# Two linear-attention blocks mixed by a gate: a second key unit by seven products, and three first products put together in PSUM

## The chip, the cores and the metric

One Trainium2 chip; the kernel uses one of its cores. The metric is the device time of one execution in microseconds (us). A core has a matrix engine (TensorE, PE in the profile, with its weight loads as PEld), a vector engine (VectorE, DVE), an activation engine (ScalarE, ACT), a general one (GpSimd, POOL) and a queue processor (SyncE, SP) that issues most transfers. Matrix products are accumulated in PSUM, which has eight banks of 512 float32 columns here; everything else that is worked on lies in SBUF.

## The reference, cut to what matters

```
x: [2048, 640] bf16,  wqkv: [640, 1920],  wo: [640, 640]   (one wqkv, wo for block A, one for block B)
g = sigmoid(x @ gate_w)                                     # one number per row
block: q, k, v = split(x @ wqkv), 32 heads of 20
       phi(t) = where(t > 0, t + 1, exp(t)) + 1e-6          # = min(exp(t), 1) + max(t, 0) + 1e-6
       kv = phi(k)^T v per head,  z = sum over rows of phi(k)
       o  = (phi(q) kv) / (phi(q) z + 1e-6)
       out = o @ wo
result = g * blockA(x) + (1 - g) * blockB(x)
```

Both blocks read the same x. The kernel never forms v: it computes phi(k)^T x (called G here), multiplies that by the value weights and by wo to get one small matrix per block, and applies it to the scaled phi(q).

## The kernel before, in words

x is 16 row tiles of 128. Because the two blocks are added up at the end, many pairs of products have the form of a 2 x 2 block product, and the kernel computes such a block product with seven products instead of eight (a Strassen form). It pays with sums of operands (on DVE, before the products) and sums of results (on DVE and ACT, between the products, because the PSUM sums are copied out, added and used again).

The stages, in the order of the matrix queue:

1. K: keys. For a tile and a block, five steps (one per 128 rows of the weights) of two matmuls each, 512 and 128 or 129 columns (`k_step`, lines 652 and 653). After the two blocks of a tile, `k_post` makes phi: ACT takes exp (line 700) and for block B also the exp of the gate column (691), DVE takes min and adds EPS (703), and then either ACT takes relu (712, 727) and DVE adds (718, 730), or DVE does both at once from PSUM (739). Which of the two is listed by hand in `RELUB` and `KRS`. Tiles 0 to `KT`-1 run in order ahead of everything; the others by the list `MAIN`. Two tiles, 2*`KU` and 2*`KU`+1, are done as one unit by seven products (`ks_unit`, lines 817 to 842); its operand sums are `kw_sums` (768, of the weights) and `kx_sums` (789, of x).
2. G: phi(k)^T x in five units (`g_unit`, products at line 1166), each by seven products named 1, 2, 5, 6, 3, 7, 4; products 1 and 2 are cut before the last pair of tiles, whose parts are steps 8 and 9. The sums over keys are made by `s_pair` (889), those over x by `t_all` (914), into the buffer TX.
3. Q and R: queries (lines 1045, 1134), Q by seven products, R directly; phi again (1075, 1078, 1088, 1090, 1092, 1145 to 1152). `QD` and `RD` list where DVE takes max and sum at once.
4. kv, wp, den: small products that make the per-block matrices and the denominators, as transfers allow.
5. O: output (line 1556), eight units by seven products, with stores.

The order of the matrix queue is the list `MAIN`, written out. A token K14A is tile 14, block A; K6.5 is product 5 of the unit of tiles 12 and 13; G3.8 is step 8 of G unit 3. DVE, ACT and the queues take their order from a planner (`Sched`) that places each operation by estimated costs when the program is built; PSUM banks and other slots are given out there too. Every operation waits on semaphores for what it reads and for the former users of its slot. A matmul that must wait holds up everything behind it, since that queue is strictly in order.

In a seven-product unit the first product serves two results. In the units of K, Q and O, ACT copies it from its PSUM bank into a second bank (for keys line 842), and the second product is accumulated there on top. In the G units of the kernel before, ACT copies it to SBUF (1194), the second product has a bank of its own, and DVE adds the two (1199).

Of the kernel before, what the change touches and what calls it, by code (L numbers as in the profile page):

```python
# [11 lines left out]
D = 640  # L12
# [31 lines left out]
HC = 320  # L44
NPU = 5
SSB = 20480
RELUB = (3, 5, 7, 9, 11, 13)
KT = 10
KU = 6
KJ = 7  # L50
KWT = 5
KRS = ("10A", "10B", "11A", "11B", "12A", "13B", "14A", "14B", "15A", "15B", "8A", "9A", "9B",)
MAIN = """K6.1 K14A K6.5 K6.2 K6.6 K14B K6.3 K6.7 K10A K10B K6.4 K11A K11B K15A K15B G3.1 G3.8 G1.1 G2.1 G0.1
G3.2 G2.8 G1.8 G1.2 G1.9 G3.9 G0.2 G0.8 G0.9 G2.2 G0.5 G0.6 G1.5 G0.3 G0.7 G1.6 G3.6 G0.4 G2.9 G2.6
G2.5 Q4.1 G1.7 G1.3 G3.5 G2.7 G1.4 Q4.6 Q4.5 G2.3 Q4.2 Q4.7 G3.3 Q4.3 G2.4 Q1.1 Q0.1 kvA X2 Q1.6
Q0.5 G3.7 Q0.2 Q0.6 Q4.4 Q1.5 Q0.7 Q1.2 G4.1 Q0.3 G4.8 Q1.7 G3.4 Q3.1 Q2.1 Q1.3 G4.2 Q3.6 Q1.4 G4.6
Q3.2 Q2.5 Q2.6 Q2.2 G4.9 Q0.4 Q3.5 Q2.3 G4.5 Q3.7 Q2.7 G4.7 Q2.4 Q3.4 G4.3 G4.4 Q3.3 wA0 dA0 R4B
wA1 LA dB0 S1 S0 kvB R4A wB0 R1A R2B R2A wB1 T1 R3A R0.1 R1B R3B R0.6 R0.5 O2.1
O3.5 R0.7 R0.2 O1.1 R0.3 O0.1 O2.2 O1.2 R0.4 O0.2 O3.1 O2.6 O1.6 O3.2 O0.5 O3.6 O3.3 O1.5 O1.7 dA1
dB1 S3 S2 O1.3 O2.5 O3.7 O2.7 O2.3 O3.4 O1.4 O2.4 O0.6 O0.3 O4.1 O7.1 O6.1 O0.7 O4.2 O5.1 O6.2  # L60
O7.2 O5.2 O4.5 O4.6 O5.5 O6.5 O5.6 O4.7 O6.6 O0.4 O6.3 O6.7 O4.3 O7.6 O7.5 O5.7 O5.3 O7.7 O7.3 O4.4
O5.4 O6.4 O7.4"""
RS = (0,)
# [247 lines left out]
def body(nc, A_x, A_wqkv, A_wo, B_x, B_wqkv, B_wo, gate_w, out, log=None):  # L311
# [463 lines left out]

    def kx_sums():
        t1, t2 = 256 * KU, 256 * KU + 128
        a11, a12, a21, a22 = [XT[:, c : c + 2, lo : lo + 128] for lo in (t1, t2) for c in (0, 2)]
        for k, in0, in1, need in (
            (1, a21, a22, ()),  # L780
            (2, a11, KX[1], (1,)),
            (5, XT[:, 4, t1 : t1 + 128], XT[:, 4, t2 : t2 + 128], ()),
            (3, a21, a11, ()),
            (4, a12, KX[2], (2,)),
        ):
            bkx[k] = Buf("kx")
            op(
                "DVE",
                lambda e, k=k, in0=in0, in1=in1: e.tensor_tensor(out=KX[k], in0=in0, in1=in1, op=ALU.subtract),
                dve2(128 if k == 5 else 256),  # L790
                ins=[bxt[2 * KU], bxt[2 * KU + 1]] + [bkx[j] for j in need],
                outs=[bkx[k]],
                name="kx",
            )
# [7 lines left out]
    def ks_unit(j):  # L802
# [36 lines left out]
        def step(n):  # L839
            if n == 1:  # L840
                mm(px, D + 1, True, [(WK["A"][:, c, :], xt(c, 0)) for c in range(2)], bx + [bwk["A", c] for c in range(2)] + [bwz])
                d[1] = op("ACT", lambda e: e.activation(psw(py, D), psw(px, D), ACT.Copy), act_cost(D), ins=[px], outs=[py], name="kfk")
            elif n == 2:
                mm(py, D, False, [(WK["A"][:, c, :], xt(c, 0)) for c in range(2, 5)], bx + [bwk["A", c] for c in range(2, 5)])
            elif n == 5:
                mm(pz, D + 1, True, [(KW[1][:, c, :], KX[1][:, c, :]) for c in range(2)] + [(WK["B"][:, 4, :], xt(4, 1))], bx + [bkw[1], bkx[1], bwk["B", 4], bgc])
                d[5] = save(s5, pz, True)
            elif n == 6:
                mm(px, D + 1, False, [(KW[2][:, c, :], KX[2][:, c, :]) for c in range(2)], [bkw[2], bkx[2]], [d[1]])
                d[2] = save(s2, px, False)  # L850
            elif n == 3:
                mm(pz, D + 1, False, [(WK["B"][:, 2 + c, :], KX[4][:, c, :]) for c in range(2)] + [(WK["B"][:, 4, :], KX[5])], [bkx[4], bkx[5], bgc] + [bwk["B", c] for c in range(2, 5)], [d[5]])
                comb(pz, s2, False)
                k_post(t1, [("A", py, "%dA" % t1 in KRS), ("B", pz, "%dB" % t1 in KRS)])
            elif n == 7:
                mm(px, D + 1, False, [(KW[3][:, c, :], KX[3][:, c, :]) for c in range(2)], [bkw[3], bkx[3]], [d[2]])
# [48 lines left out]
    def t_all(j0, j1):  # L905
        xi = bxn[2 * j0 : 2 * j1] + [bxo]

        def tt(k, in0, in1, how, need):
            b = Buf("tx%d" % k)
            for j in range(j0, j1):  # L910
                bt[k, j] = b
            s_op.append(op(
                "DVE",
                lambda e: e.tensor_tensor(out=tk(k), in0=in0, in1=in1, op=how),
                dve2((j1 - j0) * LW),
                ins=xi + [bt[n, j0] for n in need],
                outs=[b],
                name="tx",
            ))
# [30 lines left out]
    for t in range(2, KT):  # L950
# [3 lines left out]
        if t == KWT:  # L954
            kw_sums()
    t_all(0, 8)
    kx_sums()
    bgt, gtx = Buf("gtx"), []
# [72 lines left out]
    def qu_unit(p, g):  # L1031
# [33 lines left out]
        def post(X, h, pv, ins):  # L1065
# [8 lines left out]
            one = ["%d.%d%s%d" % (p, g, X, i) in QD for i in range(2)]  # L1074
            o = [op("ACT", lambda e: e.activation(EQ[:, eq.slot + h, :], pv(), ACT.Exp), act_cost(512), ins=ins, outs=[eq], name="qe")]  # L1075
            rel = dst = PQ[X, b][:, g, :]
            if not one[h]:
                o.append(op("ACT", lambda e: e.activation(rel, pv(), ACT.Relu), act_cost(512), ins=ins, outs=[pq], after=home, name="qr"))
            n = 1
            if not any(one):  # L1080
                n, dst = 2, PP[X, p][:, g, :, :]
            if any(one) or two is not None:
# [3 lines left out]

                e2 = Buf("eq2")
                op("DVE", lambda e: e.tensor_scalar(ev(), ev(), 1.0, EPS, op0=ALU.min, op1=ALU.add), dve4(512 * n), ins=[eq], outs=[e2], name="qt")
                if one[h]:
                    o.append(op("DVE", lambda e: e.scalar_tensor_tensor(dst, pv(), 0.0, ev(), op0=ALU.max, op1=ALU.add), dve1(512), ins=ins + [eq, e2], outs=[pqf], after=home, name="qs"))  # L1090
                else:
                    op("DVE", lambda e: e.tensor_tensor(out=dst, in0=dst, in1=ev(), op=ALU.add), dve2(512 * n), ins=[pq, eq, e2], outs=[pqf], name="qs")
            qu_ops[p].extend(o)
# [82 lines left out]
    def g_unit(g):  # L1176
# [454 lines left out]
    kleft = len([t for t in MAIN.split() if t[0] == "K"])  # L1631
    ks, kps, ktiles, kdone = ks_unit(KU), {}, set(), {j for j in (1, 3, 5) if 2 * j + 1 < KT}
    for tok in MAIN.split():
        sch.base = None if tok[0] == "K" else 10**5
        if tok[0] == "K":
            if tok[2] == ".":
                ks(int(tok[3]))
                if tok[3] == "4":
                    ktiles |= {2 * KU, 2 * KU + 1}
            else:  # L1640
# [4 lines left out]
                if X == "B":  # L1645
                    k_post(t, [(Y, kps[Y, t], "%d%s" % (t, Y) in KRS) for Y in XS])
                    ktiles.add(t)
            kleft -= 1
            for j in (3, 5):
                if 2 * j >= KT - 2 and j not in kdone and all(t < KT or t in ktiles for t in range(2 * j - 2, 2 * j + 2)):  # L1650
# [87 lines left out]
```

## Time and profile before

| | |
|---|---|
| median of 3 runs | 175.97 us (175.24 to 176.11) |
| the profiled execution: its time | 175.2 us |
| its span (first to last instruction) | 173.8 us |
| PE busy | 171.3 us, 1331 matmuls |
| DVE busy | 140.1 us, 246 instructions |
| ACT busy | 115.3 us |
| POOL busy | 5.3 us |
| clock granted to PE | 1.00 |

The span is what the profile covers; 1.4 us of the execution's own time lie outside it. Busy times are sums of the durations as recorded. Neighbours on an engine overlap a little (a matmul's record reaches over the start of the next), so the distance between two starts, not the duration, is what one costs on a full queue. Times of day in a trace count from the span's start.

### The profile page before, as it was taken

How to read it: one execution, taken by the hardware profiler on the slowest of the kernel's cores; microseconds unless marked ns; L12 is line 12 of the kernel's file. 1: busy time of each engine (PE TensorE's matmuls, PEld its weight loads, DVE VectorE, ACT ScalarE, POOL GpSimd, SP SyncE). 2: the span in 40 equal slices, each digit the busy share in tenths (PEclk: the TensorE clock that was granted, in tenths of full speed). 3: DMA queues.
4: the chain of work that ended last, by engine and by line, in shares of the span. 5: the costliest groups of instructions: out<-in, count | busy, mean ns of one | idle time of the engine just before them, and what ended most of it. 6: DMA issues, size and time to landing. Idle time of an engine off the chain costs nothing.

```text
span 173.8 us, 3365 instructions
## 1 busy us (share of the span) xinstructions
PE 171.3 (99%) x1331; PEld 107.6 (62%) x1331; DVE 140.1 (81%) x246; ACT 115.3 (66%) x221; POOL 5.3 (3%) x17
## 2 busy tenths in 40 slices
PE   9999999999999999999999999999999999999995
PEld 4555555555577777666566565655556667777773
DVE  2275999999999958559959889799999985899550
ACT  4378888999933332467599597956898864456324
POOL 2000000000000170000000000000000000000000
PEclk9999999999999999999999999999999999999999
DMA  6969999980000025138818003277670002460125
GB/s 187 324 122 179 220 373 366 347 160 5 0 4 0 0 42 98 38 75 72 188 20 220 4 0 75 59 204 198 232 191 3 0 3 69 115 204 4 47 102 191
DMA packets 33035, 20.59 MB, mean 118 GB/s; under 512 B 18260, under 2 KB 32892, under 8 KB 33020
## 3 DMA queue, kind: packets, MB, share of 16 engines
q1 hardware_dynamic: 32062, 19.76, 44.5%
q10 hardware_dynamic: 958, 0.63, 1.2%
q8 instruction: 10, 0.16, 0.4%
q14 instruction: 5, 0.04, 0.1%
HBM read 10.88 MB, written 4.26 MB: 87 GB/s over the span
## 4 chain that ended last, share of the span: by engine, by line
PE 99%; ACT 0%; issue 0%; DVE 0%
PE ps L1166 22%; PE ps L1556 22%; PE ps L652 18%; PE ps L1045 13%; PE ps L1134 10%; PE ps L653 5%; PE ps L817 3%; PE ps L579 1%; PE ps L1420 1%; PE ps L1346 1%; PE ps L1314 1%; PE ps L592 1%; ACT PKS L1621 0%; DVE ONE L477 0%; PE ps L629 0%
## 5 line engine op out<-in xcount | busy, mean ns | idle before, releaser
L652 PE MATMUL ps<-WKW,XT 128*128 128x512 bf16 x140 | 38.9, 381 | 0.0
L653 PE MATMUL ps<-WKW,XT 128*128 128x128 bf16 (+1 forms) x140 | 30.7, 219 | 0.0
L700 ACT ACTIVATE EKT<-ps 128x640 bf16<-128x640 f32 x31 | 21.9, 716 | 4.6 <-PE ps L653 4.1
L652 PEld LDWEIGHTS ps<-WKW,XT 128*128 128x128 bf16 x140 | 13.7, 98 | 16.6 <-DMA WKW<-in_A_wqkv_dram 0.4
L1166 PE MATMUL ps<-TX,PKS 128*128 128x321 bf16 (+1 forms) x160 | 23.8, 300 | 0.0
L1166 PEld LDWEIGHTS ps<-TX,PKS 128*128 128x128 bf16 x160 | 15.7, 98 | 7.2
L1166 PE MATMUL ps<-XN,PKS 128*128 128x321 bf16 (+1 forms) x120 | 18.2, 300 | 0.0
L1194 ACT ACTIVATE EKT<-ps 128x321 f32<-128x321 f32 (+1 forms) x15 | 6.4, 438 | 16.6 <-PE ps L1166 9.9
L1166 PEld LDWEIGHTS ps<-XN,PKS 128*128 128x128 bf16 x120 | 11.7, 98 | 5.5
L653 PEld LDWEIGHTS ps<-WKW,XT 128*128 128x128 bf16 x140 | 13.7, 98 | 0.0
L1075 ACT ACTIVATE EQ<-ps 128x512 bf16<-128x512 f32 x18 | 10.8, 601 | 3.7 <-PE ps L1045 2.9
L889 DVE TENSOR_TENSOR PKS<-PKS 128x1280 bf16<-128x1280 bf16 (+2 forms) x20 | 12.9, 683 | 0.0
L712 ACT ACTIVATE PKS<-ps 128x640 bf16<-128x640 f32 x16 | 11.4, 722 | 0.0
L703 DVE TENSOR_SCALAR EKT<-EKT 128x1280 bf16<-128x1280 bf16 (+1 forms) x19 | 8.2, 435 | 3.7 <-ACT EKT L700 3.6
L1145 ACT ACTIVATE EQ<-ps 128x1024 bf16<-128x1024 f32 x8 | 8.2, 1028 | 4.3 <-PE ps L1134 3.6
L1045 PE MATMUL ps<-XT,WQA 128*128 128x512 bf16 x36 | 10.4, 379 | 0.0
L1579 DVE TENSOR_TENSOR PKS<-ps,PKS 128x320 bf16<-128x320 f32 x11 | 5.4, 490 | 5.2 <-PE ps L1556 4.9
L1199 DVE TENSOR_TENSOR WKW<-ps,EKT 128x320 bf16<-128x320 f32 x15 | 7.2, 486 | 2.8 <-PE ps L1166 2.6
L1134 PE MATMUL ps<-XT,WQA 128*128 128x512 bf16 x40 | 9.4, 381 | 0.0
L1134 PE MATMUL ps<-XT,WQB 128*128 128x512 bf16 x40 | 9.2, 380 | 0.0
L1572 ACT ACTIVATE PKS<-ps 128x320 f32<-128x320 f32 x11 | 4.8, 441 | 5.9 <-PE ps L1556 5.9
L739 DVE SCALAR_TENSOR_TENSOR PKS<-ps,EKT 128x640 bf16<-128x640 f32 x10 | 8.2, 820 | 0.1
(179 smaller groups left out, 321.9 us busy)
## 6 DMA issues: line engine op xcount, KB each, us to landing
out_dram<-PKS SPq DMA_DIRECT2D x15, 160.0 KB, 1.8
XN<-in_A_x_dram SPq DMA_DIRECT2D x1, 2240.0 KB, 9.1
WKW<-in_A_wqkv_dram SPq DMA_DIRECT2D x5, 160.0 KB, 3.7
WKW<-in_B_wqkv_dram SPq DMA_DIRECT2D x5, 160.0 KB, 3.6
WQA<-in_A_wqkv_dram SPq DMA_DIRECT2D x1, 800.0 KB, 10.8
WQB<-in_B_wqkv_dram SPq DMA_DIRECT2D x1, 800.0 KB, 12.0
WVA<-in_A_wqkv_dram SPq DMA_DIRECT2D x1, 800.0 KB, 12.0
PKS<-in_B_wqkv_dram SPq DMA_DIRECT2D x1, 800.0 KB, 5.2
```

Source lines behind the costliest of these rows:

```text
L652: e.matmul(a[:, 0:512], l, WK[X][:, c, 0:512], start=(c == 0), stop=(c == NC - 1))
L653: return e.matmul(a[:, 512:w], l, WK[X][:, c, 512:w], start=(c == 0), stop=(c == NC - 1))
L700: op("ACT", lambda e, i=i, ps=ps: e.activation(evg(i), psg(ps), ACT.Exp), act_cost(D), ins=[ps] + first, outs=[ek, b], name="ke")
L703: lambda e: e.tensor_scalar(EK[:, ek.slot : ek.slot + n, :], EK[:, ek.slot : ek.slot + n, :], 1.0, EPS, op0=ALU.min, op1=ALU.add),
L712: op("ACT", lambda e, X=X, ps=ps: e.activation(pkt(X, t), psg(ps), ACT.Relu), act_cost(D), ins=[ps], outs=[rk], name="kr")
L739: lambda e, X=X, i=i, ps=ps: e.scalar_tensor_tensor(pkt(X, t), psg(ps), 0.0, evg(i), op0=ALU.max, op1=ALU.add),
L889: lambda e: e.tensor_tensor(out=out, in0=a, in1=b, op=ALU.subtract),
L1045: r = e.matmul(PS[:, ps.slot, :], w, x, start=(first and i == 0), stop=(i == len(prs) - 1), skip_group_check=not first)
L1075: o = [op("ACT", lambda e: e.activation(EQ[:, eq.slot + h, :], pv(), ACT.Exp), act_cost(512), ins=ins, outs=[eq], name="qe")]
L1134: r = e.matmul(PS[:, ps.slot + h, :], WQ[X][:, c, g::5], XT[:, c, 1024 + 512 * h : 1536 + 512 * h], start=(c == 0), stop=(c == NC - 1))
L1166: r = e.matmul(PS[:, ps.slot, 0:w], reg[:, j, :], mov(j, w), start=(first and j == 0), stop=(j == 7), skip_group_check=not first)
L1556: r = e.matmul(PS[:, ps.slot, 0:HALF], reg(g), mov(g), start=(first and g == 0), stop=(g == NC - 1), skip_group_check=not first)
```

## The change

- A second unit of keys by seven products: `KU` becomes (3, 6), so that tiles 6 and 7 are done like 12 and 13. `KT` falls from 10 to 4: tiles 0 to 3 run ahead, tiles 4 to 15 by `MAIN`, whose first line now begins with tiles 4, 5 and unit 3. The sums of x get a set of buffers per unit (`KX[u, k]`) and are queued after tile `KXT[u]` = 3; those of the weights after tile `KWT` = 2 instead of 5.
- `t_all`, the sums of x behind TX, is queued at the token `TXT` = K15B in two halves (eight operations of 4 x 322 columns a row instead of four of 8 x 322), and waits for the last key operation of DVE that stands before it there.
- In the G units in `FK` = (0, 1, 2), product 1 is copied by ACT from PSUM into the bank of product 2 (1274 in the changed file), product 2 runs undivided at step 9 on top of it (step 2 is empty), and ACT copies the result out (1279); DVE's addition is gone in these three.
- In the query units the wait of DVE's min step and of its addition is narrowed: where a half is done alone, it waits for the exp and relu of that half, not for both.
- The lists of who does max and sum (`RELUB`, `KRS`, `QD`, `RD`) and `MAIN` are new. The G and O products, R and the small products keep their number and sizes.

```
-KT = 10
-KU = 6
+KT = 4
+KU = (3, 6,)
-KWT = 5
+TXT = "K15B"
+FK = (0, 1, 2,)
+KXT = {3: 3, 6: 3}
+KWT = 2
-MAIN = """K6.1 K14A K6.5 K6.2 K6.6 K14B K6.3 K6.7 K10A K10B K6.4 K11A K11B K15A K15B G3.1 G3.8 G1.1 G2.1 G0.1
-G3.2 G2.8 G1.8 G1.2 G1.9 G3.9 G0.2 G0.8 G0.9 G2.2 G0.5 G0.6 G1.5 G0.3 G0.7 G1.6 G3.6 G0.4 G2.9 G2.6
...
+MAIN = """K4A K5A K3.1 K5B K3.2 K3.5 K3.6 K4B K3.7 K3.3 K10A K3.4 K8A K8B K15A K10B K15B K11A K6.1 K14A
+K6.5 K6.2 K6.6 K11B K6.3 K9A K6.7 K9B K14B K6.4 G1.1 G1.2 G0.1 G0.2 G2.1 G2.2 G0.8 G1.8 G2.8 G3.1
+G0.9 G3.2 G2.9 G1.9 G0.5 G0.6 G3.8 G3.9 G1.5 G0.3 G2.6 G1.6 G3.6 G1.3 G0.7 G2.5 G0.4 G1.7 G2.3 G3.5
...
-QD = ("0.0A0", "0.0A1", "0.1B0", "0.1B1", "0.2A0", "0.2B0", "0.2B1", "0.3A0", "1.0B1",)
-RD = ("A0", "A1", "A4", "B0",)
+QD = ("0.0A0", "0.0A1", "0.0B0", "0.1B0", "0.1B1", "0.2A0", "0.2B0", "0.3A0", "0.3B1", "0.4A1", "0.4B1", "1.0B1",)
+RD = ("A0", "A1", "A3", "A4", "B0",)
...
+                after=pk_last[-1:],
                 name="tx",
...
-    t_all(0, 8)
-    kx_sums()
+        for u in KU:
+            if t == KXT[u]:
+                kx_sums(u)
...
-                e2 = Buf("eq2")
-                op("DVE", lambda e: e.tensor_scalar(ev(), ev(), 1.0, EPS, op0=ALU.min, op1=ALU.add), dve4(512 * n), ins=[eq], outs=[e2], name="qt")
+                e2, mine = Buf("eq2"), [ex] if any(one) else exs
+                q = [op("DVE", lambda e: e.tensor_scalar(ev(), ev(), 1.0, EPS, op0=ALU.min, op1=ALU.add), dve4(512 * n), ins=mine, outs=[e2], name="qt")]
...
+        if g in FK:
+            py.need = HC
...
-            if n in (2, 9):
+            if n in (2, 9) and g not in FK:
                 prod(g, "P2", py, ra2, xv(1, False), HC, True, lambda j: xn(j, 1) + [bpk[one[0], 2 * j + 1]], js=(0, KJ) if n == 2 else (KJ, 8))
             if n == 8:
-                d["s1"] = save(t1, px, HC, "p1s")
+                if g in FK:
+                    d["s1"] = op("ACT", lambda e: e.activation(PS[:, py.slot, 0:HC], PS[:, px.slot, 0:HC], ACT.Copy), act_cost(HC), ins=[px], outs=[py], name="p1f")
+                else:
+                    d["s1"] = save(t1, px, HC, "p1s")
+            elif n == 9 and g in FK:
+                prod(g, "P2", py, ra2, xv(1, False), HC, False, lambda j: xn(j, 1) + [bpk[one[0], 2 * j + 1]])
+                op("ACT", lambda e: e.activation(GT[:, ga.slot, 0:HC], PS[:, py.slot, 0:HC], ACT.Copy), act_cost(HC), ins=[py], outs=[ga], prio=-2, name="c11")
             elif n == 9:
                 comb(ga, 0, py, t1, "c11")
...
+            if tok == TXT:
+                t_all(0, 4)
+                t_all(4, 8)
```

More of the change, by code (lines that the diff above doesn't have):

```diff
@@ L855, in step @@
             elif n == 7:
-                mm(px, D + 1, False, [(KW[3][:, c, :], KX[3][:, c, :]) for c in range(2)], [bkw[3], bkx[3]], [d[2]])
+                mm(px, D + 1, False, [(KW[3][:, c, :], KX[j, 3][:, c, :]) for c in range(2)], [bkw[3], bkx[j, 3]], [d[2]])
                 d[7] = comb(px, s5, True)
@@ L1085, in ev @@
                     return EQ[:, eq.slot : eq.slot + 2, :] if n == 2 else EQ[:, eq.slot + h, :]
[L1087 to L1088 removed]
+                e2, mine = Buf("eq2"), [ex] if any(one) else exs
+                q = [op("DVE", lambda e: e.tensor_scalar(ev(), ev(), 1.0, EPS, op0=ALU.min, op1=ALU.add), dve4(512 * n), ins=mine, outs=[e2], name="qt")]
                 if one[h]:
[L1090 to L1092 removed]
+                    q.append(op("DVE", lambda e: e.scalar_tensor_tensor(dst, pv(), 0.0, ev(), op0=ALU.max, op1=ALU.add), dve1(512), ins=ins + [e2], outs=[pqf], after=home, name="qs"))
+                    o.append(q[1])
+                else:
+                    q.append(op("DVE", lambda e: e.tensor_tensor(out=dst, in0=dst, in1=ev(), op=ALU.add), dve2(512 * n), ins=[rl if any(one) else pq, e2], outs=[pqf], name="qs"))
+                for x in q:
+                    x.ins.append(eq)
+                    eq.readers.append(x)
             qu_ops[p].extend(o)
@@ L1647, in body @@
                     ktiles.add(t)
+            if tok == TXT:
+                t_all(0, 4)
+                t_all(4, 8)
             kleft -= 1
-            for j in (3, 5):
+            for j in (1, 3, 5):
                 if 2 * j >= KT - 2 and j not in kdone and all(t < KT or t in ktiles for t in range(2 * j - 2, 2 * j + 2)):
```

63 lines of the change are left out of this document (35 added, 28 removed).

## The prediction

> **What bounds the kernel now.** I read the page first: span, busy time, clock and chain.
>
> ```profile
> span 173.8 us, 3365 instructions
> ...
> PE 171.3 (99%) x1331; PEld 107.6 (62%) x1331; DVE 140.1 (81%) x246; ACT 115.3 (66%) x221; POOL 5.3 (3%) x17
> ...
> PEclk9999999999999999999999999999999999999999
> ...
> PE 99%; ACT 0%; issue 0%; DVE 0%
> ```
>
> The chain that ended last is matmuls almost throughout, at full granted clock. A busy matmul engine could still hide waits, so next come the waits of PE:
>
> ```profile
> PE ps L579 <- DVE ONE L477: 0.3, 1, 0.3
> ```
>
> That is its only row: after the first 0.3 us no matmul waited for another engine. So every matmul that is taken away shortens the span by its distance to the next one, and every new wait of a matmul lengthens it, one for one. The price of a key step is in the timeline of PE (start, duration):
>
> ```profile
> 4.37 0.38 PE L652 MATMUL ps<-WKW,XT 128*128 128x512 bf16 x1
> ...
> 24.84 0.38 PE L652 MATMUL ps<-WKW,XT 128*128 128x512 bf16 x1
> ...
> 30.29 0.38 PE L652 MATMUL ps<-WKW,XT 128*128 128x512 bf16 x1
> ```
>
> Between the last two lie 20 steps (a 512- and a 128-column matmul each): 5.45 / 20 = 0.2725 us a step. Last, the helpers, by stage (span, then PE, PEld, DVE and ACT busy):
>
> ```profile
> 12.30:31.30 19.00, 19.00 (x141) 10.76 (x140) 16.63 (x29) 16.63 (x32) 0.00 (x0) 1.00 1.06 281
> 31.30:47.10 15.80, 15.80 (x117) 8.94 (x116) 15.71 (x26) 15.36 (x31) 0.00 (x0) 1.00 0.47 121
> 47.10:57.00 9.90, 9.90 (x75) 7.13 (x74) 9.65 (x17) 3.62 (x9) 0.00 (x0) 1.00 0.01 2
> ...
> 79.70:130.00 50.30, 50.30 (x443) 29.74 (x443) 45.26 (x81) 40.36 (x66) 0.25 (x2) 1.00 0.52 123
> ```
>
> The keys end at 47.1. Until 31.3 DVE and ACT have room (16.6 of 19.0); from there to 47.1 both are full; in the first products of G ACT is nearly free.
>
> **The change, part by part.** *Matmuls.* Tiles 6 and 7 took 2 tiles x 2 blocks x 5 = 20 steps; by seven products they take 2+3+3+2+3+2+3 = 18. That is 4 matmuls fewer (1327 against 1331), 2 x 0.2725 = 0.545 us. The other products keep number and width: step 9 of a forked G unit runs the eight matmuls that steps 2 and 9 had. The switches between products of different tile shapes are as many as before. So the gain has a hard top: 0.54 us, 0.31%. (The Trainium skill, "TensorE: Matmul & The Clock Gate", section "Back-to-back issue gap", gives 131 and 81 ns as the sustained distance of 512- and 128-column matmuls with weight loads. By it the gain would be an estimated 2 x 0.212 = 0.42 us; this trace, with 0.2725 a pair, doesn't agree.)
>
> *What the second unit puts on ACT and DVE*, by groups of one shape (count, busy, mean ns), with the pieces that the new lists move:
>
> ```profile
> L712 ACT ACTIVATE PKS<-ps 128x640 bf16<-128x640 f32 x16 | 11.4, 722 | 0.0
> ...
> L1078 ACT ACTIVATE PQ<-ps 128x512 bf16<-128x512 f32 x6 | 3.6, 594 | 0.0
> ...
> L1194 ACT ACTIVATE EKT<-ps 128x320 f32<-128x320 f32 x5 | 2.0, 438 | 4.6 <-DVE PKS L718 3.0 <-PE ps L1166 1.5
> ...
> L842 ACT ACTIVATE ps<-ps 128x640 f32<-128x640 f32 x1 | 0.7, 726 | 0.0
> L823 ACT ACTIVATE PQ<-ps 128x645 f32<-128x645 f32 x1 | 0.7, 717 | 0.0
> ```
>
> ```profile
> L889 DVE TENSOR_TENSOR PKS<-PKS 128x1280 bf16<-128x1280 bf16 x12 | 9.6, 817 | 0.0
> ...
> L1199 DVE TENSOR_TENSOR WKW<-ps,EKT 128x320 bf16<-128x320 f32 x15 | 7.2, 486 | 2.8 <-PE ps L1166 2.6
> ...
> L914 DVE TENSOR_TENSOR TX<-XN 128x2576 bf16<-128x2576 bf16 x2 | 3.0, 1494 | 0.0
> ...
> L1090 DVE SCALAR_TENSOR_TENSOR PQ<-ps,EQ 128x512 bf16<-128x512 f32 x4 | 2.8, 692 | 0.1
> ...
> L830 DVE TENSOR_TENSOR ps<-ps,PQ 128x641 f32<-128x641 f32 x1 | 0.8, 833 | 0.1
> ...
> L789 DVE TENSOR_TENSOR PQ<-XT 128x256 bf16<-128x256 bf16 x2 | 0.6, 284 | 0.0
> ```
>
> ACT gets three copies (2.2) and two more relus of keys (1.4). DVE gets two additions (1.7), four sums of 256 columns and one of 128 (1.3). None of it is in front of PE unless a queue runs late; that is worked out below.
>
> *TX sums behind the keys.* Four of 1.49 become eight halves. I take 0.82 each, from the nearest row (1280 columns, L889), so 0.6 more in all; from below, half of 1.49, nothing more. Six stand before the last key steps, two behind. From the min step of tile 9 to the 1024-column sum that G1.5 reads, DVE has nine key steps, two halves and nine pair sums. By the L889 row scaled to their widths, and less the 0.08 by which neighbours overlap, they cost 3.9 + 1.5 + 4.3 = 9.8 us. PE has 10.9 from G1.1 to G1.5: ten products and five single steps, 80 matmuls at 0.137:
>
> ```profile
> 47.16 2.08 PE L1166 MATMUL ps<-XN,PKS 128*128 128x321 bf16 x14
> ```
>
> ((2.08 - 0.30) / 13 = 0.137.) Both start near 46.6: about 1 us to spare, so I take nothing; if DVE comes 1 us late there, each further us is paid in full.
>
> *Forks in G.* Three copies into PSUM in place of three to SBUF (0.44 either way), three additions of 0.49 off DVE, three copies out (0.44) on ACT, in the stage where ACT is busy 3.6 of 9.9. G0.8's copy has 1.2 us until G0.9 (one product, two single steps). Zero; without that cover, up to 3 x 0.44.
>
> *Queries.* Three relus (0.59) leave ACT and three max-and-sums (0.69) come to DVE, with more but shorter min steps and one such exchange of double width in R: some 2.5 us more on DVE, in a stage of 50.3 us where it was busy 45.3, 2.8 less on ACT. I take zero: no matmul waited there, and the narrowed waits let DVE start earlier. How near one came is seen in the next two rows, an exp that ends at 132.05 and the matmuls that take over its bank 0.16 later, unhindered:
>
> ```profile
> 130.99 1.06 ACT L1145 ACTIVATE EQ<-ps 128x1024 bf16<-128x1024 f32 x1
> ...
> 132.21 0.84 PE L1556 MATMUL ps<-PKS,PQ 128*128 128x320 bf16 x5
> ```
>
> *Transfers.* The orders of SP and POOL hardly change. K3.1 needs tiles 6 and 7 at 17.7, nearly 3 us earlier than their direct steps did. Their transfer is the first of the two issues in the first row (the queue's timeline), and takes 5.6 to land (the tile's view at 10.5): 16.1. Hidden by 1.6.
>
> ```profile
> 10.51 5.74 SPq L445 DMA_TRANSPOSE XT<-in_A_x_dram  x2
> ```
>
> ```profile
> DMA to landing us min/median/max: 5.6/5.6/5.6
> ```
>
> *The tight place: ACT between 12.5 and 28.* Unit 3 now stands where ACT had its room. Block B of tile 8 (K8B) takes the bank that block B of tile 7 leaves, once its exp is read. Before K8B stand 87 steps: 4.37 + 87 x 0.2725 = 28.1. ACT, from the gate column of tile 2 (same place in both programs) to that exp, has 24 instructions of 640 to 645 columns and 6 gate columns. Their distances:
>
> ```profile
> 12.53 0.17 ACT L691 ACTIVATE GE<-ps 128x1 f32<-128x1 f32 x1
> ...
> 15.25 0.17 ACT L691 ACTIVATE GE<-ps 128x1 f32<-128x1 f32 x1
> 15.32 0.70 ACT L712 ACTIVATE PKS<-ps 128x640 bf16<-128x640 f32 x1
> ...
> 32.23 0.71 ACT L700 ACTIVATE EKT<-ps 128x640 bf16<-128x640 f32 x1
> 32.81 0.73 ACT L842 ACTIVATE ps<-ps 128x640 f32<-128x640 f32 x1
> 33.48 0.70 ACT L700 ACTIVATE EKT<-ps 128x640 bf16<-128x640 f32 x1
> 34.08 0.70 ACT L712 ACTIVATE PKS<-ps 128x640 bf16<-128x640 f32 x1
> ```
>
> 0.07 a gate column; 0.58, 0.67 and 0.60 for the wide ones, where 0.67 is the copy into PSUM. With 0.60: 12.53 + 24 x 0.60 + 6 x 0.07 + 0.1 (the last one's duration beyond its distance) = 27.4. To that come five short pauses in which the next input isn't there yet, 0.1 to 0.2 each by the places of the matmuls (tile 3's first block, tiles 4 and 5 first, tile 5's second, and DVE's addition after K3.7), 0.7 in all: 28.1. It meets the matmul exactly. K3.7, five us earlier, and K15A and K10B, right after, come out with 0.1 to 0.3 to spare by the same count. I put the waits at 0.2 us: between 0 (at 0.58 a piece) and 1.2 (at 0.67, where the pauses go and the later ones follow). Queued behind such a wait is the whole matmul queue.
>
> **Sum** against the profiled execution: 173.8 - 0.54 + 0.2 = 173.5 span, 174.9 with the 1.4 around it. Its own time, 175.2, is the lowest of those shown; the median is 175.97. On the median the same -0.34 gives 175.6.
>
> **Rivals.** (1) *No wait at all.* The count above is rough by 0.1 to 0.2, and the room of 0.16 in the R stage speaks for it: -0.54, 175.4 on the median. (2) *Slower: ACT becomes the bound between 12.5 and 33.* Place: the banks of K8B, K15A and K10B. Price: with 0.67 for each wide one, 24 x 0.67 + 0.5 + 12.53 = 29.1 against 28.1; ten more wide ones until 33 add 0.3 to 0.5. Net -0.54 + 1.4 = +0.9: 176.9. It decides from 0.54 us of waits up, 0.02 a piece over my 0.60. Against it: distances of 0.58 and 0.60 are the rule in the rows, 0.67 the exception. (3) *The clock.* Many short waits could drop the granted clock. The start shows what that costs:
>
> ```profile
> 3.88 0.59 PE L652 MATMUL ps<-WKW,XT 128*128 128x512 bf16 x1
> ```
>
> 0.59 instead of 0.38 from 4.37 on; the slow stretch reaches from 0.3 to 4.3, and 4 us at half rate cost 2: 177.6 on the median. Against it: the granted clock is 9 in all 40 slices. (This is the rule of the Trainium skill, "TensorE: Matmul & The Clock Gate", section "A second HAM failure mode: psum-queue depth-cycling": short idling between groups of matmuls makes the clock swing between half and full. No run here shows it yet.) (4) *The second unit saves nothing* can't be: four matmuls are gone, and none waited.
>
> **How the numbers follow.** Forecast 0.57, rival 1 0.20, rival 2 0.20, rival 3 0.03. About 0.5% (0.88 us) is what a measurement of this kernel can tell from no change: its three runs span 0.87. Faster by more than that needs the whole gain and luck of the runs: a third of rival 1 and a seventh of the forecast, 0.15. Slower: three quarters of rival 2 and rival 3, 0.18. The same: 0.67. The range goes from the lowest run less the whole gain (175.24 - 0.54 = 174.7, rounded down to 174.6) to rival 2, 176.9.
>
> **What would show it.** Right: 1327 matmuls; the first of G's products at 46.6 to 46.9 instead of 47.16; PE's waits with a row or two of at most 0.2 by ACT at L658 between 23 and 31; none by DVE before G1.5. Wrong: waits of PE on ACT above 0.6 in sum (rival 2), a wait by TX or pair sums between 55 and 62, waits in the query stage where I took none, or a slice of the granted clock below 9 (rival 3).

## The result and the profile after

The changed kernel takes 175.34 us (median of 22 executions, 174.87 to 175.89) and the kernel before, run beside it, 175.81 (22 executions, 175.24 to 176.11). The ratio is 0.9977, 95% interval 0.9967 to 0.9987: 0.4 us or 0.23% faster, by this document's bound of 0.5% no change. The forecast was 175.6, which is 0.34 us less than a median before of 175.97; beside the 175.81 measured here it is 175.47. 0.4 us less were found, with the interval from 0.23 to 0.58.

The page of the changed kernel: span, busy times, granted clock, and the chain that ended last.

```profile
span 174.1 us, 3381 instructions
...
PE 170.8 (98%) x1327; PEld 107.3 (62%) x1327; DVE 142.5 (82%) x262; ACT 115.9 (67%) x225; POOL 4.9 (3%) x17
...
PEclk9999999999999999999999999999999999999999
...
PE 96%; DMA 3%; SPq 0%; ACT 0%; issue 0%
```

Four matmuls fewer, 0.5 us of PE gone, the clock full. Yet this span is 0.3 longer than the span shown of before. The new 3% of DMA in the chain says why, and the waits of PE (total, times, longest) name it:

```profile
PE ps L658 <- DMA WKW<-in_A_wqkv_dram: 0.8, 1, 0.8
PE ps L585 <- DVE ONE L483: 0.3, 1, 0.3
```

In this execution a weight load that the third step of the first tile needs landed late. The change doesn't touch it, and such waits move between executions (0 to 0.8 in the profiles below); this execution's own time, 175.57, is 0.23 over its median, as that of before, 175.2, was 0.6 under its own. So the two traces have to be compared from a point behind the first loads. First the timeline of PE in the changed kernel (start, duration), then the same matmul, the third of the keys, in the kernel before:

```profile
5.34 0.39 PE L658 MATMUL ps<-WKW,XT 128*128 128x512 bf16 x1 [0.81 <-DMA WKW<-in_A_wqkv_dram]
...
28.50 0.38 PE L658 MATMUL ps<-WKW,XT 128*128 128x512 bf16 x1
...
28.84 0.39 PE L658 MATMUL ps<-WKW,XT 128*128 128x512 bf16 x1
...
47.36 1.39 PE L1184 MATMUL ps<-XN,PKS 128*128 128x321 bf16 x9
...
105.11 1.25 PE L1184 MATMUL ps<-TX,PKS 128*128 128x320 bf16 x8
106.42 0.60 PE L1372 MATMUL ps<-WOA,WVA 64*60 64x320 bf16 x15
```

```profile
4.67 0.39 PE L652 MATMUL ps<-WKW,XT 128*128 128x512 bf16 x1
```

From there to the first product of G: before 47.16 - 4.67 = 42.49, now 47.36 - 5.34 = 42.02. The keys are 0.47 us shorter: 0.545 for the two steps less, and a wait of 0.065 given back. That wait is at 28.84, 0.34 behind the step at 28.50 instead of 0.27. It is K8B, which takes the bank of tile 6 block B (the prediction names tile 7, but counts up to this exp); the exp that frees it is the first of the two in this row of ACT's timeline (the second starts 0.6 later; the first ends at 28.78):

```profile
28.07 1.31 ACT L706 ACTIVATE EKT<-ps 128x640 bf16<-128x640 f32 x2
```

K8B was due at 28.77. The exp ends 0.01 after that, and 0.06 more go by from its end to the matmul's start: the wait is almost all hand-over.

Behind the keys one more wait is new. The first product with the output's weights, 106.42, comes 0.135 late. Its bank is read by a z sum on DVE, which stands behind an addition of a query block:

```profile
105.70 0.41 DVE L1107 TENSOR_TENSOR PQ<-PQ,EQ 128x512 bf16<-128x512 bf16 x1
106.03 0.25 DVE L1233 SCALAR_TENSOR_TENSOR DEN<-EKT,ps,CST 128x32 bf16<-128x32 f32 x1
```

The z sum ends at 106.28, when the product is due (106.29), so this wait too is the hand-over, 0.15 us here. Neither wait is in the list of waits: both are short, and were found by the distances of PE's starts. Together: -0.545 + 0.065 + 0.135 = -0.345, against -0.34 in the prediction. By stage (span, then PE, PEld, DVE, ACT busy) the helpers have less room than before, and PE hardly feels it:

```profile
12.50:28.00 15.50, 15.50 (x117) 8.79 (x115) 14.11 (x26) 15.32 (x31) 0.00 (x0) 1.00 1.06 241
28.00:38.00 10.00, 10.00 (x75) 5.57 (x74) 9.90 (x23) 9.72 (x20) 0.00 (x0) 1.00 1.08 323
38.00:47.00 9.00, 9.00 (x67) 5.09 (x66) 8.87 (x14) 8.80 (x20) 0.00 (x0) 1.00 0.16 31
```

ACT is busy 15.32 of 15.5 us between 12.5 and 28; before, each of the two had 16.6 of 19.0 between 12.3 and 31.3.

### The profile page after: what moved, and what is told of

It reads as the page before. It is cut to its first block, busy times and chain, and to the rows that moved or that the text cites. A ratio compares the mean times of both kernels' runs of the same rounds, so it can differ in the third digit from the quotient of the medians.

```text
span 174.1 us, 3381 instructions
## 1 busy us (share of the span) xinstructions
PE 170.8 (98%) x1327; PEld 107.3 (62%) x1327; DVE 142.5 (82%) x262; ACT 115.9 (67%) x225; POOL 4.9 (3%) x17
## 4 chain that ended last, share of the span: by engine, by line
PE 96%; DMA 3%; SPq 0%; ACT 0%; issue 0%
PE ps L1184 22%; PE ps L1582 22%; PE ps L658 15%; PE ps L1056 13%; PE ps L1152 10%; PE ps L823 6%; PE ps L659 4%; DMA WKW<-in_A_wqkv_dram 3%; PE ps L1446 1%; PE ps L1372 1%; PE ps L1340 1%; SPq L451 0%; ACT PKS L1647 0%; PE ps L635 0%
## 5 line engine op out<-in xcount | busy, mean ns | idle before, releaser
L658 PE MATMUL ps<-WKW,XT 128*128 128x512 bf16 x120 | 33.9, 380 | 0.8 <-DMA WKW<-in_A_wqkv_dram 0.8
L659 PE MATMUL ps<-WKW,XT 128*128 128x128 bf16 (+1 forms) x120 | 26.3, 219 | 0.0
L706 ACT ACTIVATE EKT<-ps 128x640 bf16<-128x640 f32 x30 | 20.8, 721 | 3.4 <-PE ps L659 3.0
L658 PEld LDWEIGHTS ps<-WKW,XT 128*128 128x128 bf16 x120 | 11.8, 98 | 15.1 <-DMA WKW<-in_A_wqkv_dram 1.1
L718 ACT ACTIVATE PKS<-ps 128x640 bf16<-128x640 f32 x18 | 12.8, 724 | 0.0
L1214 ACT ACTIVATE EKT<-ps 128x321 f32<-128x321 f32 (+1 forms) x12 | 5.2, 438 | 11.2 <-PE ps L1184 5.6
L659 PEld LDWEIGHTS ps<-WKW,XT 128*128 128x128 bf16 x120 | 11.8, 98 | 0.0
L1065 ACT ACTIVATE PKS<-ps 128x512 f32<-128x512 f32 x12 | 7.0, 602 | 4.1 <-PE ps L1056 4.1
L1219 DVE TENSOR_TENSOR WKW<-ps,EKT 128x320 bf16<-128x320 f32 x12 | 5.8, 485 | 3.1 <-PE ps L1184 3.0
L724 DVE TENSOR_TENSOR PKS<-PKS,EKT 128x1280 bf16<-128x1280 bf16 x9 | 7.4, 817 | 0.1
L1605 DVE TENSOR_TENSOR PKS<-ps,EKT 128x320 bf16<-128x320 f32 x7 | 3.4, 491 | 4.7 <-PE ps L1582 2.7
## 6 DMA issues: line engine op xcount, KB each, us to landing
WQB<-in_B_wqkv_dram SPq DMA_DIRECT2D x1, 800.0 KB, 12.3
```

Source lines behind the costliest of these rows:

```text
L658: e.matmul(a[:, 0:512], l, WK[X][:, c, 0:512], start=(c == 0), stop=(c == NC - 1))
L659: return e.matmul(a[:, 512:w], l, WK[X][:, c, 512:w], start=(c == 0), stop=(c == NC - 1))
L706: op("ACT", lambda e, i=i, ps=ps: e.activation(evg(i), psg(ps), ACT.Exp), act_cost(D), ins=[ps] + first, outs=[ek, b], name="ke")
L718: op("ACT", lambda e, X=X, ps=ps: e.activation(pkt(X, t), psg(ps), ACT.Relu), act_cost(D), ins=[ps], outs=[rk], name="kr")
```

## The experiments

Each kernel is the changed one with the edit shown. None leaves any part of the computation out; where an operation is repeated, it writes the same values again. Times are medians. "Against the change" is the difference of the two ratios to the kernel before, times 175.8 us; by the intervals it is known to 0.3 or 0.4 us, for e5, e6 and e11 to 0.5 to 0.7.

| run | us | ratio to before (95%) | against the change |
|---|---|---|---|
| the change | 175.34 | 0.9977 (0.9967 to 0.9987) | |
| e1, unit 3 direct | 175.49 | 0.9998 (0.9984 to 1.0012) | +0.4 |
| e2, one exp more on ACT | 176.15 | 1.0030 (1.0015 to 1.0044) | +0.9 |
| e3, two copies more on ACT in G | 175.27 | 0.9979 (0.9968 to 0.9991) | 0.0 |
| e4, one relu less on ACT | 176.42 | 1.0043 (1.0026 to 1.0060) | +1.2 |
| e5, TX sums behind the keys | 182.10 | 1.0362 (1.0335 to 1.0390) | +6.8 |
| e6, two forks undone | 179.22 | 1.0215 (1.0189 to 1.0242) | +4.2 |
| e7, query lists undone | 177.02 | 1.0074 (1.0053 to 1.0094) | +1.7 |
| e8, as e4, TX sums split | 175.47 | 0.9988 (0.9975 to 1.0001) | +0.2 |
| e9, three forks undone, product late | 177.00 | 1.0074 (1.0060 to 1.0089) | +1.7 |
| e10, new keys with the old order behind | 178.72 | 1.0175 (1.0159 to 1.0191) | +3.5 |
| e11, six TX halves behind the keys | 180.33 | 1.0236 (1.0198 to 1.0274) | +4.6 |

### The gain by itself: e1

```
-KU = (3, 6,)
+KU = (6,)
-KXT = {3: 3, 6: 3}
+KXT = {6: 3}
-MAIN = """K4A K5A K3.1 K5B K3.2 K3.5 K3.6 K4B K3.7 K3.3 K10A K3.4 K8A K8B ...
+MAIN = """K4A K4B K5A K5B K6A K6B K7A K7B K10A K8A K8B ...
```

> Tiles 6 and 7 directly again (20 steps, no operand sums, no copies for them), all else as in the changed kernel. Theory (the matmul queue bounds, four matmuls are the gain): 1331 matmuls, plus 0.545 us, less the 0.07 that the wait before K8B cost, so 0.45 to 0.55 longer than the changed kernel; against the kernel before 0.9977 + 0.003 = 1.000 to 1.002. Rival (the gain comes from the new lists, the forks or the moved sums, and unit 3 only shifts work): stays at 0.997 to 0.998.

Measured: +0.4 us (0.1 to 0.7 by the intervals), with no wait in the keys. The wait at the first product with the output's weights is gone as well, so the trace gives 0.545 - 0.065 - 0.135 = 0.345. With the moved sums, the forks and the lists all left in, the ratio to the kernel before is 0.9998: the four matmuls are the gain, and nothing else is.

### The tight place on ACT: e2 and e3

e2 does one exp of tile 4 twice, right ahead of the tight place; e3 does one copy of G unit 0 three times.

```
+                if (t, X) == (4, "A"):
+                    op("ACT", lambda e, i=i, ps=ps: e.activation(evg(i), psg(ps), ACT.Exp), act_cost(D), ins=[ps], outs=[ek, b], after=ke, name="ke")
```

```
-                op("ACT", ... GT[:, ga.slot, 0:HC], PS[:, py.slot, 0:HC], ACT.Copy ... name="c11")
+                c11 = []
+                for _ in range(3 if g == 0 else 1):
+                    c11 = [op("ACT", ... ACT.Copy ... after=c11, prio=-2, name="c11")]
```

> The exp of tile 4, block A is done twice (the same values written again): one wide ACT instruction more, 0.6 to 0.7 us of its queue, right in the stretch that ends with the exp before K8B. Theory (ACT has no room left there): the matmuls wait 0.5 to 0.7 us more in sum before K3.2 to K8B, and the time is longer by the same, 1.001 to 1.002 of the kernel before. Rival (the wait of 0.07 is a local matter of one bank, and ACT has hidden room): 0.997 to 0.998, starts of G unmoved.

> The copy out of the first product sum of G unit 0 is done three times: 0.7 us more of ACT's queue, but in the G stage, where it was nearly free. Theory: no matmul waits, 0.997 to 0.998 of the kernel before, as without it. Rival (ACT's total decides, wherever it is spent): 0.6 us longer, 1.001.

e2 measured +0.9 us for one instruction whose neighbours start 0.58 apart. Its trace has no single place where that is paid. By the distances of PE's starts it is 0.08 at 19.8, 0.11 at 23.4, 0.09 at 32.5, 0.10 at 37.3, 0.31 at 45.0 and 0.36 at 47.5, in sum 1.05; the two waits of the changed kernel, 0.2, are absent, which leaves 0.85. The last one alone shows in the timeline of PE:

```profile
47.16 0.43 PE L825 MATMUL ps<-WKW,XT 128*128 128x512 bf16 x2
47.80 0.43 PE L1186 MATMUL ps<-XN,PKS 128*128 128x321 bf16 x2 [0.20 <-DVE PKS L726]
```

Of the 1.05, 0.46 (37.3 and 47.5) are waits for DVE, which was full already at the end of the keys, and 0.59 are waits for ACT. In G the same engine has room: two copies more (e3) cost nothing.

### Less for ACT, and slower: e4 and e8

If ACT is the narrow engine, one relu less in front of the tight place should help or do nothing. DVE then does max and sum of that block at once.

```
-KRS = (... "4A", "4B", "5A", "5B",)
+KRS = (... "4A", "5A", "5B",)
```

> Tile 4, block B gives its relu to DVE (max and sum in one from PSUM): ACT 0.6 us less before K8B, DVE 0.4 us more. Theory: the start of K8B follows its forerunner at 0.27 instead of 0.34, the 0.07 are gone; DVE had 0.4 to spare in the tightest place behind (before K6.5), so nothing new or up to 0.1; time the same within 0.1 us, 0.997 to 0.998. Rival (the wait before K8B isn't ACT's load): the 0.34 stays.

Measured: +1.2 us, which neither theory had. The wait at K8B is gone as expected, and three others came: 0.36 at K8A (27.6), 0.53 at 45.7 and 0.58 at 48.4. The first, by L745, is the moved step itself: K8A takes the bank of tile 4 block B, which now comes free when DVE's max and sum is done. Waits of PE in e4:

```profile
PE ps L1184 <- DVE PKS L724: 0.4, 1, 0.4
PE ps L658 <- ACT EKT L706: 0.4, 1, 0.4
...
PE ps L658 <- DVE PKS L745: 0.2, 1, 0.2
```

The timeline of DVE holds a cause for the two late ones. In the changed kernel four halves of the TX sums stand in front of the addition that product 6 of unit 6 leads to (L836). In e4 the planner, with other due times, put a fifth one and a min step ahead of it. First the changed kernel, then e4:

```profile
41.38 0.82 DVE L920 TENSOR_TENSOR TX<-XN 128x1288 bf16<-128x1288 bf16 x1
42.18 0.83 DVE L836 TENSOR_TENSOR ps<-ps,PQ 128x641 f32<-128x641 f32 x1
```

```profile
42.48 0.83 DVE L920 TENSOR_TENSOR TX<-XN,TX 128x1288 bf16<-128x1288 bf16 x1
43.22 0.49 DVE L709 TENSOR_SCALAR EKT<-EKT 128x1280 bf16<-128x1280 bf16 x1
43.62 0.83 DVE L836 TENSOR_TENSOR ps<-ps,PQ 128x641 f32<-128x641 f32 x1
```

The addition comes 1.44 us later (0.2 of it because the whole matmul queue runs that much later there), and everything of unit 6 behind it. Either that order made the late waits, or DVE had no room for the half us that max and sum cost it more. e8 tells the two apart. It is e4 to the instruction, with the second four halves put into the list later:

```
             if tok == TXT:
                 t_all(0, 4)
+            if tok == "K11B":
                 t_all(4, 8)
```

> As the run in which one relu of tile 4 was taken off ACT (176.42, with waits of 0.36 at 27.6, 0.53 at 45.7 and 0.58 at 48.4), but the second four halves of the TX sums are put into the list four steps later, behind block B of tile 11, so that again four and not five of them stand in front of the addition that K6.6 waits for, as in the changed kernel; the work of DVE is the same to the instruction. Theory A (the place of the sums among the late key steps made the waits): the two late waits go, the one at 27.6 stays, 0.3 us over the changed kernel: 175.6. Theory B (DVE has no room for the 0.55 us more, wherever it lies): 0.5 to 1.1 us of waiting by DVE stays between 38 and 60: 176.0 to 176.4.

Waits of PE in e8, and its row of the addition:

```profile
PE ps L658 <- DMA WKW<-in_A_wqkv_dram: 0.5, 1, 0.5
...
PE ps L658 <- DVE PKS L745: 0.2, 1, 0.2
```

```profile
42.37 0.83 DVE L836 TENSOR_TENSOR ps<-ps,PQ 128x641 f32<-128x641 f32 x1
```

Both late waits are gone and the 0.36 at K8A stays; less the 0.2 of the changed kernel's own two waits, which are absent here, that is 0.16, and the time is 0.2 over the change. The late waits were the order, not the load. Before an edit of one entry is judged, one has to see what the planner made of the rest.

### The TX sums: e5 and e11

```
-TXT = "K15B"
+TXT = "K6.4"      # e5: all eight halves behind the last key step
+TXT = "K11B"      # e11: two among the key steps, six behind
```

> All eight halves of the TX sums stand behind the last key step on DVE, nothing else is changed. In the changed kernel six of them lie among the key steps (39.15 to 47.4), and the last sum that the first TX product of unit 1's step 5 needs ends 0.66 us ahead of it (0.06 of that is the hand-over). Theory of the prediction (about 1 us to spare there, each further us paid in full): six halves of 0.74 move behind, 4.4 us; DVE finishes the key steps at most 0.7 earlier, as the last exp on ACT ends at 49.7; less the 0.6 to spare leaves a wait of 3.1 us by DVE at the products of G between 56 and 59: about 178.5 us. Rival: DVE has more room behind the keys than the row of 0.66 tells, because the pair sums and the other sums can be dealt out otherwise: no more than 1 us, 176.3.

> The TX sums come into the list four steps later (behind block B of tile 11), so that DVE does two halves among the key steps and six behind them, instead of six and two. With all eight behind there were waits of 0.56, 1.22 and 2.88 between 52 and 62, and the matmuls after them ran at half rate for 3 us. Theory: two halves fewer behind the keys than there, 1.48 less of waiting, and the pair sum that stood ahead of the last key addition may go too (0.5): 2.2 to 3.2 us of waiting at the TX products; no half rate, since a single wait of 3.5 us in another run brought none: 177.4 to 178.5. Rival for the clock: waits of 2 to 3 us in sum within 6 us bring the half rate as well: 1.6 us more, 179 to 180.

Waits of PE in e5, then in e11:

```profile
PE ps L1184 <- DVE PKS L895: 2.7, 1, 2.7
PE ps L1184 <- DVE TX L920: 1.1, 1, 1.1
...
PE ps L1184 <- DVE PKS L736: 0.4, 1, 0.4
```

```profile
PE ps L1184 <- DVE PKS L895: 2.7, 1, 2.7
```

By the distances of the starts these are 4.7 us in e5 (3.1 expected) and 2.9 in e11 (2.2 to 3.2 expected). In e5 a pair sum also slipped in front of the last key addition (the 0.4), and DVE didn't get through the key steps sooner without the TX sums, since those wait for exps. So the step in the prediction is confirmed in kind: behind the keys DVE has less than a us to spare, and what goes beyond it is paid. It isn't a clean measure of the price, because the planner dealt the sums anew: the long waits stand in step 5 of unit 0 (matmuls at 56.35 and 56.62 in the changed kernel), not in step 5 of unit 1, for which the prediction counted. There, in the changed kernel, the spare is 0.66 less the hand-over of 0.06. The second sum of its DVE row, of 1024 columns, ends at 56.72 + 0.88 = 57.60, and the product that reads it starts at 58.26:

```profile
56.72 0.88 DVE L895 TENSOR_TENSOR PKS<-PKS 128x256 bf16<-128x256 bf16 x2
```

```profile
58.26 0.44 PE L1184 MATMUL ps<-TX,PKS 128*128 128x321 bf16 x2
```

The rest is the clock: in each of the two traces thirteen matmuls at half rate cost 1.7 us. e11 by windows cut at its own events (span, PE, PEld, DVE, ACT, POOL busy, then the granted clock):

```profile
56.90:59.70 2.80, 0.13 (x1) 0.00 (x0) 2.80 (x6) 0.00 (x0) 0.00 (x0) 1.00 0.00 0
59.70:61.00 1.30, 1.27 (x9) 0.90 (x10) 1.30 (x5) 0.44 (x1) 0.00 (x0) 0.95 0.00 0
61.00:64.20 3.20, 3.20 (x13) 1.81 (x12) 2.82 (x5) 0.77 (x2) 0.00 (x0) 0.50 0.00 0
64.20:66.00 1.80, 1.80 (x15) 1.25 (x13) 0.56 (x2) 0.44 (x1) 0.00 (x0) 0.98 0.00 0
```

PE waits 2.8 us, runs 1.3 us at full rate, then 3.2 us at half. Five of e11's six executions have a mean clock of 0.99 (179.64 to 180.59); one has 1.00 and took 178.04, which is the theory's number without the drop. So e11's row of the table mixes both. Of e5's six, three have 0.99 (181.41 to 181.86) and three 0.98 (182.34 to 182.78). My rival for the clock was right, and "a single wait of 3.5 us in another run brought none" was a rule made from one trace: of e6's six executions two, not profiled, have 0.99 as well.

### The forks: e6 and e9

```
-FK = (0, 1, 2,)
+FK = (2,)         # e6
```

> Units 0 and 1 of G again by copies to SBUF and additions on DVE, unit 2 with its three first products put together in PSUM as in the changed kernel: two additions of 0.49 us more on DVE between 55 and 62, the copies of ACT as many as before. Theory: the forks cost and bring nothing by themselves as long as the sums for the first TX products keep their 0.6 us; by 0.49 or 0.98 more in front of them the spare goes and 0 to 0.4 us of waiting comes: 175.3 to 175.7, and what is seen is a wait by DVE at the products between 57 and 60 or none. Rival: the copy into PSUM stands in the way of the matmuls of step 9, so that without two of them the time falls: 175.0 or less.

+4.2 us; I had expected 0 to 0.4. Part of it is the clock in the two executions with 0.99; the four with 1.00, at 178.67 to 179.32, are 3.8 over the change. Waits of PE in e6 (the profiled execution is one of the four; by the starts the wait is 3.5):

```profile
PE ps L1184 <- DVE PKS L736: 3.4, 1, 3.4
```

The wait is at 48.0, at step 2 of unit 1. In a forked unit step 2 is empty and its seven matmuls run at step 9. Without the fork they stand where the list has the token, and ask for the odd tiles' keys, the last of which DVE finishes at 51.4 (in the changed kernel at 51.8). So the fork's first effect here is not an addition saved but a product moved behind the last key steps. e9 takes that effect away: no forks at all, with the step 2 tokens moved to right ahead of step 9.

```
-FK = (0, 1, 2,)
+FK = ()
-... G1.1 G1.2 G0.1 G0.2 G2.1 G2.2 G0.8 G1.8 G2.8 G3.1 G0.9 G3.2 G2.9 G1.9 ...
+... G1.1 G0.1 G2.1 G0.8 G1.8 G2.8 G3.1 G0.2 G0.9 G3.2 G2.2 G2.9 G1.2 G1.9 ...
```

> All three forks undone, but the second product of units 0, 1 and 2 (step 2, seven matmuls) stands right ahead of step 9, where the changed kernel has it with the forks; with two forks undone and step 2 left at its old place a matmul waited 3.4 us at 48.0 for the additions of the last key tiles (179.22). PE's list is then that of the changed kernel; DVE has three additions of 0.49 us more (0.41 apart), and they stand in front of the sum that the first TX products need, which had 0.6 us to spare. Theory A (the place of the product was what the run before paid for): 3 x 0.41 - 0.6 = 0.6 us of waiting by DVE between 56 and 59: 175.9. Theory B (the forks as such save what was seen): a wait of 2 us or more between 47 and 53: 177.5 to 179.2.

Waits of PE in e9:

```profile
PE ps L1152 <- DVE WVA L1387: 0.8, 1, 0.8
PE ps L1184 <- DVE PKS L895: 0.7, 2, 0.5
```

The wait of 3.4 is gone: the place of the product was it. Between 57 and 59 there are 1.07 us of waits by the starts, where 0.6 was expected. DVE does the three additions ahead of the pair sums, 0.41 each, and for one of them it waits 0.40 for its product; 3 x 0.41 + 0.40 - 0.60 = 1.03. The other wait, at 108.6 (0.67 when a matmul missing from the record is taken off), is behind the queries, whose DVE order the planner also dealt anew; what made L1387 late there is left open. So the forks are worth about 1 us here by the additions that they take off DVE in front of the first TX products, and 3.4 (e6's wait) by where their product runs.

### The query lists, and the new keys with the old order: e7 and e10

```
-QD = ("0.0A0", "0.0A1", "0.0B0", "0.1B0", ... "0.3B1", "0.4A1", "0.4B1", "1.0B1",)
-RD = ("A0", "A1", "A3", "A4", "B0",)
+QD = ("0.0A0", "0.0A1", "0.1B0", "0.1B1", "0.2A0", "0.2B0", "0.2B1", "0.3A0", "1.0B1",)
+RD = ("A0", "A1", "A4", "B0",)
```

> The two lists of the query stage as in the kernel before (three single relus go back from DVE to ACT, and one of double width in R), the rest as in the changed kernel, the narrowed waits too. Theory: nothing in this stage is on the path, so 175.3 with 0.2 either way; the wait of 0.135 at the first product with the output's weights (106.42), which an addition of a query block on DVE causes, may go or come elsewhere. Rival: the 2.5 us that were moved to DVE are what makes that wait, and others hidden below the rows: at least 0.3 faster. Other rival: ACT is the narrow one there: 0.5 or more slower, with waits on ACT between 70 and 105.

Waits of PE in e7:

```profile
PE ps L1056 <- ACT PKS L1065: 0.5, 1, 0.5
PE ps L1152 <- ACT XT L1169: 0.4, 1, 0.4
...
PE ps L1446 <- DVE PQ L1107: 0.3, 1, 0.3
```

+1.7 us, and two of the three rows are by ACT: the second rival, ACT is the narrow one there. By the starts it is four waits, 1.7 us in sum: 0.64, 0.25 and 0.48 by ACT, 0.34 by DVE. The window from 80 to 106 in e7, the changed kernel and the kernel before:

```profile
80.00:106.00 26.00, 25.44 (x139) 14.72 (x138) 19.96 (x43) 23.73 (x48) 0.25 (x2) 1.00 0.37 73
```

```profile
80.00:106.00 26.00, 26.00 (x145) 15.56 (x144) 23.00 (x53) 22.63 (x45) 0.25 (x2) 1.00 0.35 76
```

```profile
80.00:106.00 26.00, 26.00 (x194) 16.05 (x186) 22.08 (x48) 21.14 (x42) 0.25 (x2) 1.00 0.42 78
```

The old lists in the new order put 23.73 us of ACT work there, against 21.14 in the kernel before with the same lists: the new order of the query steps brings more of it into this window, and the new lists take 1.1 off again. (The three windows don't hold the same matmuls: 139, 145 and 194, most of the surplus being the small ones of kv.) e10 turns it round: the new keys and the forks, with the order of G, queries and output of the kernel before, and its lists.

```
-MAIN = """K4A ... K6.4 G1.1 G1.2 G0.1 G0.2 ...     (the changed order)
+MAIN = """K4A ... K6.4 G3.1 G3.8 G1.1 G2.1 ...     (keys as changed, the rest as before)
+QD and RD as in e7
```

> The key part of the changed kernel and its forks, with the order of G, the queries and the output of the kernel before and its two lists of the query stage. With the changed order and the old lists there were 1.4 us of waits in the query stage (177.02). Theory A (lists and order are dealt out for each other; in the order of before nothing waited with the old lists): no wait over 0.2 between 70 and 130; what the forked units pay at the start of G, where unit 3's first products stand ahead of the others, is 0 to 1.5, since step 2 of unit 3 and the early single steps ask for the last key tiles sooner: 175.4 to 176.8. Theory B (in the changed kernel ACT is late in the query stage whatever the order, because the matmuls come 0.5 us sooner): waits on ACT of 0.5 or more between 70 and 125 again: 176.5 to 178.

Waits of PE in e10:

```profile
PE ps L1184 <- DVE PKS L745: 1.7, 1, 1.7
PE ps L1184 <- ACT ps L1274: 1.3, 2, 0.7
```

The other rows of that view, 0.2 each, are holes in the record, where the row of a matmul is missing; there is no real wait between 70 and 130, so theory A holds for the queries: lists and order belong together. The price at the start of G was more than I had allowed, 3.5 us in sum of the starts (1.91 at 47.7, 0.87 at 53.8, 0.75 at 56.1) against 0 to 1.5. The eighth matmul of the products, step 8 of unit 3, asks for the last key tiles too soon, and the copies into PSUM of the forked units are late for an order that wasn't laid out for them. No run undoes the halving of the TX sums or the narrowed waits of the query units, so what those two are worth is not shown.

## Why the prediction was right, point by point

- *Matmuls, -0.545, every one on the path.* Right: 42.49 to 42.02 us in the keys, less a wait of 0.065; e1 gives +0.4 back. The estimate by the Trainium skill ("TensorE: Matmul & The Clock Gate", section "Back-to-back issue gap"), 0.42, would with the same wait make the keys 0.36 shorter; the trace has 0.47.
- *The tight place on ACT, 0.2.* The place was right to the matmul: K8B, and the exp that frees its bank (of tile 6 block B; I wrote tile 7). I had both at 28.1; with the start 0.67 later (5.34 against 4.67) that is 28.77, and the exp ends at 28.78. The size was 0.065, nearly all of it the 0.06 from the end of the exp to the start of the matmul, for which my count had no term. It recurs, 0.06 to 0.07, in e3, e5, e6, e7, e9, e10 and e11. e2 shows how near the edge it is: one piece of 0.58 more costs 0.9, as rival 2 had it (it "decides from 0.54 us of waits up").
- *The sum, -0.34.* The trace has -0.345, but part of this is luck: 0.135 of the waits stand in the query stage, where I took none, and are caused by DVE. "Waits in the query stage where I took none" was on my own list of what would be wrong.
- *TX sums, about 1 us to spare, nothing paid.* Nothing is paid. The spare was 0.6, not 1 (my terms add up to 9.7, where I wrote 9.8). Of the three terms the two halves (1.48) and the nine pair sums (4.43) came out near the 1.5 and 4.3 counted, but the nine key steps take 51.70 - 47.41 = 4.29, not 3.9: two of them are max and sum at once from 640 columns (L745), as long as an addition of 1280 columns. e5 and e11 show that what goes beyond the spare is paid, and that the clock adds its part.

```profile
47.41 0.89 DVE L709 TENSOR_SCALAR EKT<-EKT 128x1280 bf16<-128x1280 bf16 x2
...
49.35 0.81 DVE L745 SCALAR_TENSOR_TENSOR PKS<-ps,EKT 128x640 bf16<-128x640 f32 x1
...
51.70 0.82 DVE L920 TENSOR_TENSOR TX<-XN 128x1288 bf16<-128x1288 bf16 x1
```

- *Forks, zero.* Right as a cost (e3: ACT has room in G), but not seen for what they do. "Three additions of 0.49 off DVE" is worth 1 us just there (e9), because the spare behind the keys is 0.6. And "step 9 of a forked G unit runs the eight matmuls that steps 2 and 9 had" was read as a count only; where it runs is worth 3.4 us (e6).
- *Queries, zero.* Right within 0.135. The reason given, that no matmul waited there before, holds for the order before only; in the new order the lists are worth 1.7 us (e7).
- *Transfers, zero.* Right for the tiles: K3.1 didn't wait. The late weight load at the start isn't the change's.
- *"The first of G's products at 46.6 to 46.9".* It stands at 47.36, because of that load: a time of day in one execution was the wrong measure, a distance from a matmul behind the loads the right one.
- *The rivals.* No wait at all (175.27 beside the 175.81 measured before) fits the median as well as the forecast does (175.47), and only the trace, with its two waits, decides for the forecast. ACT as the bound did not come; e2 is how it looks. The clock did not drop; e11 and e5 show it dropping behind waits of 2.8 us and more, and 3.2 us at half rate cost 1.7 there, in keeping with my 2 for 4 us. Changing DVE's share and not ACT's is what decided most of the runs, and no rival named DVE.

## What to carry to other kernels

Where the bottleneck engine's queue is full, a change is worth the instructions it takes off that queue, and only if the lists that feed it are dealt out again. Here 0.5 us of matmuls were won, and parts of the re-dealing that were priced at zero cost 1.7 to 6.8 us when they were undone or moved. A step that is free in the whole change isn't free by itself: ask what stands late if it is left out, and from which spare (0.6 us here) it draws. And where two engines are counted out to meet exactly, count the hand-over too (0.06 to 0.15 us here). When work moves off one engine, read the order of the other engines in the built program before believing that it is a relief.

## What was not expected of the hardware

- A single wait of the matmul queue of 2.8 us was followed, 1.3 us after it had ended, by 3.2 us at half the clock (e11's profile; five executions of six have the lower mean clock and took 1.6 to 2.6 us more than the sixth). Waits of 3.5 us in e6 did so in two of six executions (mean clock 0.99; 179.98 and 180.04 against 178.67 to 179.32), 4.7 us in three pieces in e5 in all six. Waits of up to 1.9 us (e10) did so in none, nor did six short ones in e2. The Trainium skill ("TensorE: Matmul & The Clock Gate", section "What's actually happening") has an activity window of about 3.4 us that runs freely, and half rate after an idle one. The length of the half rate, 3.2, and the chance from one execution to the next agree with such a window; that the wait must fill 3.4 us doesn't agree with e11.
- The start isn't the same from one execution to the next. The first weight loads held PE up by 0.8 us in the profile of the change, 0.5 in e8 and not at all in e1; in e1 instead the half rate lasted to 5.8 us (matmuls 0.53 apart in pairs where 0.27 is usual), 1.5 us longer than in the kernel before:

```profile
4.76 0.63 PE L658 MATMUL ps<-WKW,XT 128*128 128x512 bf16 x1
...
5.29 0.63 PE L658 MATMUL ps<-WKW,XT 128*128 128x512 bf16 x1
```

- Handing over from ACT or DVE to a matmul that was held up took 0.06 us where the matmul waits for one semaphore (K8B; the product at 67.03 of the changed kernel; three in e5), and 0.15 where it waits for two or three (the product at 106.42; 47.80 in e2; 48.68 in e4). Waits this short don't show as waits, only as distances.
